# Crossbar transposes, v scaled on GpSimd, and a list-scheduled order, in a fused linear attention and squared-ReLU FFN

## The chip, the cores and the metric

One core of a Trainium2 chip. The metric is the device time of one execution in microseconds. A run is called slow when it lies over 1.5% above the fastest run of the same kernel; only fast runs are compared here unless it is said otherwise. Engines: PE is TensorE, ACT is ScalarE, DVE is VectorE, POOL is GpSimd, SP is the sync engine, which here only issues DMAs.

## The reference

The attention is linear, with a feature map of two exponentials. Its output is the FFN's input.

```python
# q, k, v: (8, 8, 576, 64); w_phi: (64, 128); w_in: (512, 2048); w_out: (2048, 512)
def phi(x):
    proj = np.einsum('bhsd,df->bhsf', x, w_phi)
    proj = proj - np.max(np.abs(proj), axis=-1, keepdims=True)
    return np.concatenate([np.exp(proj), np.exp(-proj)], axis=-1)
q_p, k_p = phi(q), phi(k)
kv = np.einsum('bhsf,bhsd->bhfd', k_p, v);  z = np.sum(k_p, axis=2)
num = np.einsum('bhsf,bhfd->bhsd', q_p, kv)
den = np.einsum('bhsf,bhf->bhs', q_p, z)[..., None] + 1e-06
x = (num / den).transpose(0, 2, 1, 3).reshape(4608, 512)
h = np.maximum(x @ w_in, 0.0);  return (h * h) @ w_out
```

## The kernel before

Attention runs batch by batch (8 batches of 576 tokens), the FFN chunk by chunk (9 chunks of 512 tokens). The FFN of chunk c is merged, in program order, with the attention of batch c + 1. Per batch, attention does this: load k, q and v with a cast to bf16 (POOL); transpose k and q on PE through one PSUM buffer; project; take the absolute maximum (DVE) and the exponentials of k (ACT); scale v by exp of the maximum (DVE); accumulate kv; build the features of q with the maximum subtracted by a small matmul; divide; transpose x on PE; copy x^T out of PSUM (ACT).

```python
for tg in tgroups:                                    # k and q: PE transpose, DVE copy
    for x, xt, tag in ((xk, kT, "kT"), (xq, qT, "qT")):
        tp = ps.tile([P, 2, 512], BF16, tag="tp", bufs=1, name="tp")
        ...
                nc.tensor.transpose(out=dst, in_=src, identity=ident)
        nc.vector.tensor_copy(out=t[:, : len(tg), :w], in_=tp[:, : len(tg), :w])
...
nc.vector.tensor_copy(out=mp[:, :, 0:NI], in_=mq)     # the split of the maximum of q
nc.vector.tensor_tensor(
    out=mp[:, :, NI : 2 * NI], in0=mq, in1=mp[:, :, 0:NI], op=ALU.subtract)
...
    nc.vector.tensor_tensor(                          # v scaled
        out=o[:, :, :, :D], in0=v0,
        in1=o[:, :, :, D].to_broadcast([P, 4, 4, D]), op=ALU.mult)
...
    nc.tensor.transpose(                              # x
        out=xtp[:, c, :m], in_=xo[:m, c * P : (c + 1) * P], identity=ident[:m, :m])
nc.scalar.activation(out=xT[ch][:, :, col : col + m], in_=xtp[:, :, :m], func=ACT.Copy)
...
def ffn_in(c, mc):                                    # 16 per chunk
    ... 4 matmuls of 128x512 ...
    nc.scalar.activation(out=hr, in_=hp, func=ACT.Relu)
    nc.vector.tensor_tensor(out=t, in0=hr, in1=hr, op=ALU.mult)
...
for c in range(NCH + 1):
    ...
    merge(a, 44, steps(ffn_units(c)), 16 if c in (0, NCH) else 32)
```

## Time and profile before

| | before |
|---|---|
| median of 4 runs | 458.7 us (458.1 to 459.3) |
| PE / DVE / ACT / POOL busy | 394.7 / 267.1 / 252.0 / 34.0 us of 457.1 |
| first FFN matmul | 54.9 us |
| PE busy from 120 to 320 us | 182.8 of 200 us |

The first fence has lines of the profile's page of the kernel before: busy time of each engine with its share of the span and its instructions; then the span in 40 slices of 11.4 us, where a digit is the busy share in tenths (PEclk is the granted PE clock in tenths of full speed); then the chain of work that ended last, by engine.

```profile
PE 394.7 (86%) x4320; PEld 211.2 (46%) x4376; DVE 267.1 (58%) x465; ACT 252.0 (55%) x377; POOL 34.0 (7%) x58
...
PE   0646799799888998899899989998999899999975
...
PEclk9996599999999999999999999999999999999999
DMA  8999514410641154116412540110111112021122
...
PE 49%; DVE 29%; ACT 14%; issue 4%; DMA 2%; POOL 1%; ACTq 0%; another core or an unknown queue 0%; DVEq 0%; POOLq 0%
```

The second is the busy time by windows. After the window come its length and the busy time of PE, PE weight loads, DVE, ACT and POOL, each with its number of instructions, then the granted clock, the DMA share and GB/s.

```profile
core 0: us, PE busy (x) PEld busy (x) DVE busy (x) ACT busy (x) POOL busy (x), PEclk, DMA share, GB/s
0.00:50.00 50.00, 23.74 (x358) 17.01 (x358) 24.13 (x36) 19.79 (x25) 15.60 (x28) 0.89 1.10 189
50.00:100.00 50.00, 44.38 (x528) 24.13 (x535) 31.36 (x55) 31.12 (x49) 3.66 (x6) 0.91 0.30 51
120.00:320.00 200.00, 182.83 (x2293) 99.03 (x2321) 137.29 (x237) 128.55 (x193) 12.31 (x20) 1.00 0.28 52
```

PE is what the kernel is bound by, once it has started: from 120 to 320 us it is busy for 182.8 of 200 us. (Of 4376 matmuls, as the weight loads count them, 4320 are recorded, so busy times of PE may be a few us low; FFN matmuls without gaps come every 0.22 us, so 28 missing in these 200 us are up to 6.) In the first 50 us it works less than half of the time, because batch 0's attention has nothing to be merged with.

The third is DVE's timeline where batch 0 splits the maximum of q: two instructions of 0.2 us.

```profile
27.74 0.18 DVE L175 CAST mpack_95<-mq 128x36 bf16<-128x36 f32 x1
27.96 0.20 DVE L176 TENSOR_TENSOR mpack_95<-mq,mpack_95 128x36 bf16<-128x36 f32 x1
```

### The profile page before, as it was taken

To read this page: it belongs to the slowest core of one execution; us is meant where nothing else is said; L and a number is where in the kernel's file an instruction comes from. 1 tells how busy PE (TensorE), PEld (TensorE's weight loads), DVE (VectorE), ACT (ScalarE), POOL (GpSimd) and SP (SyncE) were. 2 spreads that over 40 slices of the span, in tenths; PEclk is the share of its full clock that TensorE was granted. 3 is DMA by queue.
4 is the path that set the end of the run, shared out by engine and by line. 5 is a ranking of instruction groups with operands and counts; after the bars stand their busy time and mean duration, and the time that the engine had idled before them with its cause. 6 is when DMAs were issued, how large, how long until landed. Compare 5 with 4: busy or idle time off the path is not lost.

```text
span 457.1 us, 9984 instructions
## 1 busy us (share of the span) xinstructions
PE 394.7 (86%) x4320; PEld 211.2 (46%) x4376; DVE 267.1 (58%) x465; ACT 252.0 (55%) x377; POOL 34.0 (7%) x58
## 2 busy tenths in 40 slices
PE   0646799799888998899899989998999899999975
PEld 0434454555455545454555455545554554444432
DVE  2881279628953895389547963796469643333221
ACT  1445458466856574747674757485738474333300
POOL 8220020102010201020102010000000000000000
PEclk9996599999999999999999999999999999999999
DMA  8999514410641154116412540110111112021122
GB/s 121 215 204 207 91 25 81 77 24 10 113 81 24 22 107 77 24 30 123 76 24 40 112 65 13 33 39 1 24 24 24 26 24 47 23 48 25 45 46 68
DMA packets 21612, 28.47 MB, mean 62 GB/s; under 512 B 2112, under 2 KB 16448, under 8 KB 21568
## 3 DMA queue, kind: packets, MB, share of 16 engines
q0 software_dynamic: 15808, 18.39, 24.9%
q1 hardware_dynamic: 5760, 9.44, 8.5%
q8 instruction: 34, 0.56, 0.5%
q14 instruction: 10, 0.08, 0.1%
HBM read 36.77 MB, written 9.44 MB: 101 GB/s over the span
## 4 chain that ended last, share of the span: by engine, by line
PE 49%; DVE 29%; ACT 14%; issue 4%; DMA 2%; POOL 1%; ACTq 0%; another core or an unknown queue 0%; DVEq 0%; POOLq 0%
PE op L331 18%; PE hp L312 16%; DVE mk L153 5%; PE wide L280 4%; DVE mq L153 4%; DVE vp L202 4%; DVE vn L202 4%; ACT hr L317 3%; DVE xo L289 3%; ACT qp L242 3%; PE tp L129 3%; ACT qn L242 3%; PE xtp L297 2%; PE wide L144 2%; PE wide L258 2%
## 5 line engine op out<-in xcount | busy, mean ns | idle before, releaser
L312 PE MATMUL hp<-xT,win 128*128 128x512 bf16 x546 | 150.0, 383 | 2.8 <-issue 1.6
L317 ACT ACTIVATE hr<-hp 128x512 bf16<-128x512 f32 x144 | 86.0, 607 | 83.3 <-PE hp L312 72.4
L312 PEld LDWEIGHTS <-win 128*128 128x128 bf16 x576 | 52.0, 98 | 55.6 <-issue 2.1
L165 ACT ACTIVATE kp<-wide 128x1024 bf16<-128x1024 f32 (+1 forms) x40 | 37.5, 939 | 36.3 <-DVE mk L153 36.1
L242 ACT ACTIVATE qp<-wide 128x1024 bf16<-128x1024 f32 (+1 forms) x40 | 37.5, 937 | 34.2 <-PE wide L228 34.2
L153 DVE TENSOR_REDUCE mk<-wide 128x8 f32<-128x1024 f32 (+1 forms) x40 | 44.5, 1113 | 4.6 <-PE wide L144 4.6
L153 DVE TENSOR_REDUCE mq<-wide 128x8 f32<-128x1024 f32 (+1 forms) x40 | 44.4, 1110 | 0.5 <-PE wide L144 0.4
L337 DVE COPY ot<-op 128x512 f32<-128x512 f32 x36 | 24.8, 688 | 29.7 <-PE op L331 28.3
L242 ACT ACTIVATE qn<-wide 128x1024 bf16<-128x1024 f32 (+1 forms) x40 | 37.6, 941 | 0.0
L166 ACT ACTIVATE kn<-wide 128x1024 bf16<-128x1024 f32 (+1 forms) x40 | 37.5, 938 | 0.0
L280 PE MATMUL wide<-kv_sb,qp 128*128 128x65 bf16 (+1 forms) x320 | 31.8, 200 | 2.9 <-ACT qp L242 2.9
L287 DVE RECIPROCAL rden<-wide 128x8 f32<-128x8 f32 (+1 forms) x40 | 8.1, 204 | 42.7 <-PE wide L280 42.4
L280 PE MATMUL wide<-kv_sb,qn 128*128 128x65 bf16 (+1 forms) x320 | 26.8, 200 | 4.4 <-ACT qn L242 4.2
L280 PEld LDWEIGHTS <-qp 128*128 128x128 bf16 (+1 forms) x320 | 23.9, 103 | 12.7 <-ACT qp L242 8.4
L280 PEld LDWEIGHTS <-qn 128*128 128x128 bf16 (+1 forms) x320 | 23.2, 104 | 14.2 <-ACT qn L242 13.2
L289 DVE TENSOR_TENSOR xo<-wide,rden 128x512 bf16<-128x512 f32 (+1 forms) x40 | 27.5, 689 | 1.2
L303 ACT ACTIVATE xT<-xtp 128x512 bf16<-128x512 bf16 (+1 forms) x40 | 22.1, 552 | 4.7 <-PE xtp L297 4.3
L266 ACT ACTIVATE kv_sb<-wide 128x520 bf16<-128x520 f32 x16 | 9.4, 604 | 23.4 <-PE wide L258 23.4
L297 PE MATMUL xtp<-ident,xo 128*128 128x128 bf16 (+1 forms) x160 | 15.9, 225 | 7.0 <-DVE xo L289 6.1
L144 PE MATMUL wide<-wphi_70,kT 64*128 64x128 bf16 x288 | 16.6, 229 | 4.9 <-DVE mq L153 4.4
L67 POOL DMA_DIRECT2D xk<-in_k_dram x16 | 10.1, 637 | 144.2 <-PE tp L129 80.4
L129 PE MATMUL tp<-ident,xk 128*128 128x128 bf16 (+1 forms) x160 | 13.1, 231 | 8.7 <-POOL ident masks.py:199 8.1
(481 smaller groups left out, 612.6 us busy)
## 6 DMA issues: line engine op xcount, KB each, us to landing
out_dram<-ot SPq DMA_DIRECT2D x72, 128.0 KB, 2.4
xk<-in_k_dram POOLq DMA_DIRECT2D x16, 288.0 KB, 4.9
xq<-in_q_dram POOLq DMA_DIRECT2D x16, 288.0 KB, 6.6
xv<-in_v_dram POOLq DMA_DIRECT2D x16, 288.0 KB, 5.5
win<-in_moe_w_in_dram POOLq DMA_DIRECT2D x1, 2048.0 KB, 18.1
wout<-in_moe_w_out_dram POOLq DMA_DIRECT2D x1, 2048.0 KB, 28.7
wphi_70<-in_w_phi_dram POOLq DMA_DIRECT2D x2, 16.0 KB, 1.9
```

The lines of the kernel that those rows point to most:

```text
L129: nc.tensor.transpose(out=dst, in_=src, identity=ident)
L144: nc.tensor.matmul(out=pj[:, e, i * Fd : (i + 1) * Fd], lhsT=xt[r, i * P : (i + 1) * P], rhs=wphi2[r, :], start=True, stop=True,)
L153: nc.vector.tensor_reduce(out=m[:, :, at : at + w], in_=pj[:, :, : w * Fd].rearrange("x e (i f) -> x e i f", f=Fd), axis=AX.X, op=ALU.max, ...
L165: nc.scalar.activation(out=kp[:, :, :w], in_=pj[:, :, :w], func=ACT.Exp, scale=1.0)
L166: nc.scalar.activation(out=kn[:, :, :w], in_=pj[:, :, :w], func=ACT.Exp, scale=-1.0)
L202: nc.vector.tensor_tensor(out=o[:, :, :, :D], in0=v0, in1=o[:, :, :, D].to_broadcast([P, 4, 4, D]), op=ALU.mult,)
L242: nc.scalar.activation(out=o, in_=i_, func=ACT.Exp, scale=sg)
L280: nc.tensor.matmul(out=ndv[:m, h, : D + 1], lhsT=qph[s][:, h, :m], rhs=kv_sb[:, s, h % 2, h // 2, :], start=(s == 0), stop=(s == 1),)
L289: nc.vector.tensor_tensor(out=xo[:m].rearrange("t (h d) -> t h d", h=8), in0=ndv[:m, :, :D], in1=rden[:m].to_broadcast([m, 8, D]), op=ALU. ...
L312: nc.tensor.matmul(out=hp, lhsT=win[:, kc, mc * P : (mc + 1) * P], rhs=xT[c][:, kc, :], start=(kc == 0), stop=(kc == KC1 - 1),)
L317: nc.scalar.activation(out=hr, in_=hp, func=ACT.Relu)
L331: nc.tensor.matmul(out=op, lhsT=h2[c, mc][:, tt * P : (tt + 1) * P], rhs=wout[:, mc, :], start=(mc == 0), stop=(mc == KC2 - 1),)
```

## The change

The intent: take all transposes but a tiny one off PE, with their PSUM buffer and their copies (DVE for q and k, ACT for x); take v's scaling off DVE; and let a list scheduler in the kernel, with a cost for each operation, fix the order on every engine, so that the attention of two batches overlaps the FFN. A token order (pr, j) makes the transposes plain, and all buffers are static.

```diff
-                        nc.tensor.transpose(out=dst, in_=src, identity=ident)
-                nc.vector.tensor_copy(out=t[:, : len(tg), :w], in_=tp[:, : len(tg), :w])
+                    nc.sync.dma_start_transpose(
+                        out=xt.t[:, u0 // 2 : (u0 + n) // 2, :],
+                        in_=xb.t[:, u0 : u0 + n, :].rearrange("x u d -> x (u d)"),
+                    )
 ...
-                nc.vector.tensor_tensor(out=o[:, :, :, :D], in0=v0, ...)
+                    nc.gpsimd.tensor_tensor(
+                        out=t.t[:, us, :D], in0=xv.t[:, us, :],
+                        in1=t.t[:, us, D].to_broadcast([P, M, D]), op=ALU.mult)
 ...
-                nc.tensor.transpose(out=xtp[:, c, :m], ...)
-            nc.scalar.activation(out=xT[ch][:, :, col : col + m], in_=xtp[:, :, :m], func=ACT.Copy)
+                    nc.sync.dma_start_transpose(out=xT.t[:, tt], in_=xo.t)
 ...
+    r_xk = ring("xk", 1, [P, U, D], BF16)         # was two buffers
+    r_xq = ring("xq", 1, [P, U, D], BF16)         # was two buffers
+    r_wide = ring("wide", 2, [P, 2, 512], F32, ps)
 ...
+    def load(key, kb, fn, deps=(), bufs=()):
+        i = pl.op("pool", 650, key, fn, deps, bufs, lat=0)
+        return pl.op("dma", kb * 2.5, key, None, [i], bufs, lat=2200)
+    def xbar(key, kb, fn, deps=(), bufs=()):      # the list's costs in ns: 100 to issue, 4 per KB, 2300 to land
+        i = pl.op("sp", 100, key, fn, deps, bufs, lat=0)
+        return pl.op("xb", kb * 4, key, None, [i], bufs, lat=2300)
 ...
+    def place(b):                                 # a batch's attention over 64 FFN slots of the list;
+        if b == 0:                                # an FFN chunk is 32 slots
+            return lambda i: -200 + i
+        return lambda i: 32 * b - 24 - 64 * (1 - i / 100)
 ...
+        for o in pl.order():
+            if o.fn is not None:
+                o.fn()
```

## The prediction

> **What bounds the kernel now.** TensorE. The engine table gives PE busy 394.7 of 457.1 us, DVE 267.1, ACT 252.0, GpSimd 34.0; the chain of waits is 49% PE, 29% DVE, 14% ACT. Three stretches (busy time by windows, timeline of PE):
> - 0 to 55 us: batch 0's attention alone, a DVE/ACT latency chain, under loads that keep the DMA engines full (207 to 215 GB/s) to about 50 us. First FFN matmul at 54.9 us.
> - 55 to about 390 us: attention and FFN merged, PE 92% busy (147.3 of 160 us from 160 to 320), a batch about 45 us. The granted clock is 0.5 from 40 to 60 us, then 1.0.
> - the rest: FFN alone, 0.216 us per matmul.
>
> **What changes.**
> - Off PE: 480 transposes (xk, xq, xo). Eight take about 0.65 us warm (13.1 us busy for 160): some 30 us, and their waits (6.1 us on xo).
> - Off ACT: xT copies, 22 us. Off DVE: kT/qT copies 26.6 us, v scaling 45 us.
> - Added: 80 crossbar transposes of q and k, 36 of x, on the sync queue, 14 MB. [...] They fit the idle DMA time after 50 us; before it they share with the loads.
> - Added on GpSimd: 32 products of 128x1152. [...]
> - Moved: attention of two batches overlaps the FFN, without round trips through the single transpose PSUM buffer, and ends earlier; the FFN-only tail is about 75 us. FFN, projections, features, kv and num/den matmuls are unchanged.
>
> **Prologue.** PE's fixed order puts batch 1's first k projection before batch 0's numerators, and that load now comes after w_out. At 210 GB/s it lands at about 38 to 41 us[...]. The first FFN matmul stays at 50 to 57 us; I expect almost nothing here.
>
> **Sum.** FFN 1152 x 0.216 = 249 us; attention PE work of batches 1 to 7 about 7 x 10.3 = 72; start 54; end 3: 378 us with no stall. Before, the same sum with transposes was 406 and the run 457: 51 us lost to waits and clock. I expect 32 lost[...]. **Predicted 410 us, 8 in 10 between 388 and 438.** Faster by over 2%: 0.88; within: 0.08; slower: 0.04.
>
> **What would show it.** PE busy falls to 355 to 370 us, over 88% busy from 60 to 330 us; first FFN matmul between 50 and 57 us; DVE near 195 us[...]; PE's waits on transposes below 10 us in all.
>
> **What would make it wrong.** Transposes that land in 5 us or more would hold every projection and every chunk's first FFN matmul, in an order that cannot adapt. The fixed GpSimd order (loads behind products, products behind loads) could starve a batch. [...]

The sum in it is made of times from the profile before: 249 + 72 + 54 + 3 = 378 us with no stall. With 32 us for waits, the estimate from the 51 us lost before, it came to 410. Terms are cut from the text where a cut is marked, because no trace before the change showed them: the time of a crossbar transpose (which also stood in the estimate for the prologue), the length of a GpSimd product, and the squarings held by GpSimd, for which the author charged PE 10 to 20 of the 32 us, with the two totals that hung on them. "Warm" in it: eight transposes take 1.01 us at the start of the trace before (8.08 us) and 0.61 later (152.74).

## The result, and the profile after

The changed kernel takes 522.4 us (517.8 to 524.6, 4 runs, all fast), 1.138 times the time before (95% interval 1.129 to 1.146). Ratios are the mean time of one kernel's fast runs over that of the other's of the same rounds, so they are not quite the ratio of the medians.

| | before | after |
|---|---|---|
| median | 458.7 us | 522.4 us |
| PE / DVE / ACT / POOL busy | 394.7 / 267.1 / 252.0 / 34.0 us | 374.7 / 235.1 / 230.0 / 102.2 us |
| first FFN matmul | 54.9 us | 89.7 us |
| PE busy from 120 to 320 us | 182.8 us, clock 1.00 | 144.1 us, clock 0.85 |

The first FFN matmul: all w_in matmuls before (shortest, median and longest in ns, then the first and the last start: 54.9 and 433.6 us), and the first of them after (start, duration, engine, line, operation; in brackets what it waited for, in us):

```profile
L312 PE MATMUL hp<-xT,win x546: 376/379/634, 54.9 to 433.6; 128*128 128x512 bf16 x182
89.70 1.87 PE L484 MATMUL hp_146<-xT_106,win 128*128 128x512 bf16 x4 [5.86 <-DMA xT_106<-xo_103]
```

The same lines of the page of the kernel after (a slice is 13.0 us here):

```profile
PE 374.7 (72%) x3850; PEld 195.0 (37%) x3896; DVE 235.1 (45%) x368; ACT 230.0 (44%) x337; POOL 102.2 (20%) x90
...
PE   0002553779733866699647976899799899999996
...
PEclk9999999989955998789968997999899999999998
DMA  8999795532497216901684056903431031311123
...
PE 46%; ACT 14%; DMA 12%; DVE 12%; issue 8%; SPq 6%; POOL 1%; DVEq 0%; ACTq 0%; POOLq 0%
```

And the same windows:

```profile
0.00:50.00 50.00, 3.78 (x56) 2.56 (x57) 8.74 (x10) 7.21 (x7) 10.79 (x21) 1.00 1.07 168
50.00:100.00 50.00, 26.16 (x381) 17.68 (x377) 18.76 (x29) 22.64 (x30) 14.48 (x14) 1.00 0.73 116
120.00:320.00 200.00, 144.09 (x1623) 76.07 (x1637) 101.83 (x143) 97.27 (x143) 45.34 (x36) 0.85 0.48 79
```

Work did leave PE, DVE and ACT, but PE idles more than it saved: 3.8 us of work in the first 50, and 144 us from 120 to 320. The granted clock is 0.85 in that stretch; its lowest two slices (5 tenths) are those in which PE is busy for 3 tenths only. DMA and the sync queue are new in the chain of work that ended last (12% and 6%). From 400 us on, when loads and most of attention are over, PE is busy without gaps; so the loss lies before that.

Three places show what the new waits look like. The first is the sync queue at the start (start, duration, queue, line, operation; x5 is five transposes of batch 0, merged):

```profile
7.92 18.30 SPq L267 DMA_TRANSPOSE kT_71<-xk_67  x5
26.34 16.54 SPq L267 DMA_TRANSPOSE qT_72<-xq_68  x5
```

Ten transposes take 35 us, and this is the critical chain (start, duration, what) in that stretch:

```profile
9.33 1.49 SPq L267
...
10.86 7.30 SPq L267
...
18.20 6.71 SPq L267
...
30.47 14.70 DMA qT_72<-xq_68
```

The queue holds one transpose for 1.49 us (9.33; 1.2 to 1.5 in the second place below), the one after it for 7.30, the next for 6.71, and one of q lands 14.7 us after its issue (30.47). The five of k land 12.4 to 21.2 us after theirs. In these 50 us the DMA engines are full with the loads of the weights (the DMA line above: 8 and 9 tenths).

The second is batch 2, from 144 us, again the critical chain:

```profile
144.80 1.24 SPq L267
...
146.09 1.54 SPq L267
...
147.68 1.35 SPq L267
...
149.08 1.35 SPq L267
...
150.53 1.19 SPq L267
...
151.82 2.63 DMA xT_107<-xo_104
...
155.74 9.44 DMA xT_107<-xo_104
...
165.31 1.86 PE hp_146 L484 x4
```

Five transposes of k stand in the queue before the x transposes, for 6.9 us, then an x transpose lands after 9.44 us, and the FFN chunk (165.31) can only start behind it. POOL had issued the loads of the next batch at 154.7 us. Over all x transposes the landing goes from 2.4 to 10.3 us.

The third is DVE in batch 4, at the same two small instructions as before, and POOL beside them:

```profile
255.43 0.25 DVE L343 CAST mpack_98<-m_94 128x36 bf16<-128x36 f32 x1
255.71 9.12 DVE L344 TENSOR_TENSOR mpack_98<-m_94,mpack_98 128x36 bf16<-128x36 f32 x1
```

```profile
256.30 4.27 POOL L331 TENSOR_TENSOR va_86<-xv_69,va_86 128x1152 bf16<-128x1152 bf16 x2
260.51 4.26 POOL L331 TENSOR_TENSOR va_87<-xv_69,va_87 128x1152 bf16<-128x1152 bf16 x2
```

The subtraction, 0.2 us before, lasts 9.12 us: as long as all four products of POOL, which run from 256.3 to 264.8 (times on POOL are rough). This is the worst of eight: five of the others last 2.06 to 2.12 us, the length of one product, and two stay at 0.20. DVE does nothing else meanwhile, and the q features of that batch and the division of another wait.

So there are three candidates: the crossbar (beside loads, and in the queue), the products on GpSimd, and the order itself.

### The profile page after: what moved, and what is told of

It is laid out like the page before. It is cut to its first block, busy times and chain, and to the rows that moved or that the text cites. A ratio compares the mean times of both kernels' runs of the same rounds, so it can differ in the third digit from the quotient of the medians.

```text
span 521.8 us, 9278 instructions
## 1 busy us (share of the span) xinstructions
PE 374.7 (72%) x3850; PEld 195.0 (37%) x3896; DVE 235.1 (45%) x368; ACT 230.0 (44%) x337; POOL 102.2 (20%) x90
## 3 DMA queue, kind: packets, MB, share of 16 engines
HBM read 36.77 MB, written 9.44 MB: 89 GB/s over the span
## 4 chain that ended last, share of the span: by engine, by line
PE 46%; ACT 14%; DMA 12%; DVE 12%; issue 8%; SPq 6%; POOL 1%; DVEq 0%; ACTq 0%; POOLq 0%
PE hp_146 L484 10%; PE hp_147 L484 9%; PE op_148 L506 8%; PE op_149 L506 7%; SPq L267 6%; DVE m_96 L289 3%; DMA qT_72<-xq_68 3%; DMA xT_106<-xo_104 3%; ACT qph_92 L416 3%; DMA xT_108<-xo_105 2%; DMA xT_107<-xo_104 2%; DVE m_95 L289 2%; ACT qph_93 L416 2%; PE wide_145 L445 2%; PE wide_145 L372 2%
## 5 line engine op out<-in xcount | busy, mean ns | idle before, releaser
L219 POOL DMA_DIRECT2D xq_68<-in_q_dram x16 | 9.9, 628 | 186.2 <-DMA qT_72<-xq_68 109.9
L484 PE MATMUL hp_146<-xT_107,win 128*128 128x512 bf16 x96 | 26.2, 398 | 9.7 <-DMA xT_107<-xo_104 8.0
L445 PEld LDWEIGHTS <-qph_92 128*128 128x128 bf16 (+1 forms) x320 | 28.0, 116 | 13.3 <-issue 10.9
L445 PEld LDWEIGHTS <-qph_93 128*128 128x128 bf16 (+1 forms) x320 | 27.4, 114 | 13.2 <-issue 12.2
L484 PE MATMUL hp_146<-xT_106,win 128*128 128x512 bf16 x96 | 26.9, 406 | 6.3 <-DMA xT_106<-xo_103 5.9
L283 PEld LDWEIGHTS <-kT_71 64*128 64x128 bf16 x288 | 10.2, 101 | 55.7 <-DMA kT_71<-xk_67 28.3
L488 ACT ACTIVATE hr_110<-hp_146 128x512 bf16<-128x512 f32 x24 | 14.8, 616 | 34.1 <-PE hp_146 L484 34.1
L484 PE MATMUL hp_146<-xT_108,win 128*128 128x512 bf16 x96 | 26.3, 399 | 4.6 <-DMA xT_108<-xo_105 4.6
L283 PE MATMUL wide_144<-wphi_61,kT_71 64*128 64x128 bf16 x144 | 8.5, 239 | 29.1 <-DMA kT_71<-xk_67 21.9
L331 POOL TENSOR_TENSOR va_86<-xv_70,va_86 128x1152 bf16<-128x1152 bf16 x8 | 17.0, 2148 | 57.6 <-ACT va_86 L326 57.6
L484 PE MATMUL hp_147<-xT_106,win 128*128 128x512 bf16 x96 | 26.4, 400 | 0.2 <-ACT hr_111 L488 0.2
L331 POOL TENSOR_TENSOR va_86<-xv_69,va_86 128x1152 bf16<-128x1152 bf16 x8 | 17.1, 2161 | 47.1 <-ACT va_86 L326 47.1
L488 ACT ACTIVATE hr_111<-hp_146 128x512 bf16<-128x512 f32 x24 | 14.7, 614 | 26.1 <-PE hp_146 L484 26.1
L484 PE MATMUL hp_147<-xT_107,win 128*128 128x512 bf16 x96 | 25.6, 390 | 0.3 <-ACT hr_109 L488 0.2
L484 PE MATMUL hp_147<-xT_108,win 128*128 128x512 bf16 x96 | 25.5, 390 | 0.0
L488 ACT ACTIVATE hr_109<-hp_146 128x512 bf16<-128x512 f32 x24 | 14.8, 616 | 23.6 <-PE hp_146 L484 22.3
L289 DVE TENSOR_REDUCE m_94<-wide_144 128x8 f32<-128x1024 f32 (+1 forms) x14 | 15.0, 1070 | 20.8 <-PE wide_144 L283 19.6
L416 ACT ACTIVATE qph_92<-wide_144 128x1024 bf16<-128x1024 f32 (+1 forms) x22 | 20.9, 952 | 2.7 <-PE wide_144 L409 2.7
L513 DVE COPY ot_142<-op_148 128x512 f32<-128x512 f32 x18 | 12.4, 689 | 21.4 <-PE op_148 L506 21.4
L513 DVE COPY ot_143<-op_149 128x512 f32<-128x512 f32 x18 | 12.4, 688 | 20.7 <-PE op_149 L506 20.7
L416 ACT ACTIVATE qph_93<-wide_144 128x1024 bf16<-128x1024 f32 (+1 forms) x22 | 21.1, 961 | 0.0
```

What stands on the lines that cost most here:

```text
L219: nc.gpsimd.dma_start(out=buf.t[hi * 64 : hi * 64 + 64].rearrange("p (pr j) d -> p pr (j d)", j=NJ), in_=rows[hi],)
L283: nc.tensor.matmul(out=w.t[:, e, i * Fd : (i + 1) * Fd], lhsT=xt.t[r, u0 // 2 + i, :], rhs=wphi2[r, :], start=True, stop=True,)
L289: nc.vector.tensor_reduce(out=mb.t[:, :, u0 // 2 : (u0 + n) // 2], in_=w.t[:, :, : n * 64].rearrange("x e (i f) -> x e i f", f=Fd), axis=A ...
L331: nc.gpsimd.tensor_tensor(out=t.t[:, us, :D], in0=xv.t[:, us, :], in1=t.t[:, us, D].to_broadcast([P, M, D]), op=ALU.mult)
L416: nc.scalar.activation(out=qph[s].t[:, :, :, u0 * 32 : (u0 + n) * 32].rearrange("f hi e c -> f e hi c"), in_=w.t[:, :, : n * 64].rearrange ...
L445: nc.tensor.matmul(out=nd[lo:hi_, h, : D + 1], lhsT=qph[s].t[:, h % 2, u % 2, c0 : c0 + hi_ - lo], rhs=kv[h // 4][0].t[:, h % 2, h // 2 % ...
```

## The experiments

Every kernel here gave a correct result, unless it is said that it is wrong. Where transposes are "on TensorE" in the list order, they go through one PSUM buffer with a DVE copy for q and k and an ACT copy for x, as before; the second PSUM buffer of the FFN's output is given up for it. All these runs, and the crossbar run of experiment 6 on the 438 us kernel, also claim both feature buffers of k before a projection, which the change does not (`two = [Buf(r_kph), Buf(r_kph)]`); no run separates that.

### 1. The parts apart, in the order of the change

TensorE transposes in the list order, v on GpSimd:

```diff
+    r_op = ring("op", 1, ...);  r_tp = ring("tp", 1, [P, 8, P], BF16, ps)
-                    nc.sync.dma_start_transpose(out=xt.t[...], in_=xb.t[...])
+                        nc.tensor.transpose(out=w.t[:, i, :], in_=xb.t[...], identity=ident)
+                d_ = dve(..., nc.vector.tensor_copy(out=xt.t[...], in_=w.t[...]))
-                    nc.sync.dma_start_transpose(out=xT.t[:, tt], in_=xo.t)
+                        nc.tensor.transpose(out=w.t[:, c_, :], in_=xo.t[...], identity=ident)
+                act(..., nc.scalar.activation(out=xT.t[:, tt], in_=w.t[...], func=ACT.Copy))
```

> The list order with all transposes (q, k, x) back on TensorE through one PSUM bank, v still scaled on GpSimd. Theory A (the crossbar is the cost: slow landings beside loads, and 1.2 us of sync queue per transpose in an order that planned 0.1): 425 to 450 us, first FFN matmul near 55 us. Theory B (GpSimd products that hold up VectorE are the cost): still 490 us or more. Theory C (the fixed order itself is the cost, whatever runs in it): still 490 or more.

The same, and v on VectorE, so that of the change the order, the token layout and the static buffers are left:

```diff
-                    nc.gpsimd.tensor_tensor(
+                    nc.vector.tensor_tensor(
```

> The list order alone: transposes on TensorE and v scaled on VectorE, as before, with the flat token order and static buffers kept. A: 420 to 445 us. B: about 440 to 460. C: 480 or more, that is, slower than before although all operations are those of before.

The change with only v put back on VectorE (the same one-line edit, crossbar kept):

> The changed kernel with v scaled on VectorE, crossbar kept. A: 490 to 515 us, the first FFN matmul still at about 85 to 90 us, and the x transposes that run beside loads still land in 9 to 10 us. B: 450 to 470 us. C: about 520. In all, the longest split subtraction on VectorE should drop from 9.1 us to about 0.2.

Measured in the same rounds (before: 458.3 us), medians of four fast runs:

| list order, 64 slots | v on VectorE | v on GpSimd |
|---|---|---|
| transposes on TensorE | 480.9 (1.051) | 496.6 (1.085) |
| transposes on the crossbar | 491.6 (1.072) | 522.4 (1.138, the change; its own rounds) |

None of the three theories stands alone. The order by itself, with every operation on its old engine, costs 22.6 us (480.9 less 458.3). GpSimd adds 15.7 to that, the crossbar 10.8, and both together 41.5, which is 15.0 more than the two alone.

Where the time goes shows when each profiled run is split at its first FFN matmul:

| us to the first FFN matmul, and from there to the end | v on VectorE | v on GpSimd |
|---|---|---|
| transposes on TensorE | 63.9 and 415.0 | 68.2 and 426.8 |
| transposes on the crossbar | 85.5 and 405.4 | 89.7 and 432.1 |

The crossbar costs 21.5 us before the FFN starts in both columns. After that it gains 10 us with v on VectorE, and costs 5 with v on GpSimd: the 15.0 of "both together" lie after the first FFN matmul.

Theory A (the crossbar is the cost) had expected 420 to 445 for the order alone, so it fell; so did B and C as the only cause. In the run with v on VectorE the subtraction is back at 0.196 us (mean of 8), and the x transposes still take up to 9.7 us to land.

### 2. The crossbar without load traffic

The change, in the same order on PE, ACT and SP, with nearly no loads (the two memsets are added work on VectorE); the result is wrong:

```diff
-nc.gpsimd.dma_start(out=win, in_=win_v)
-nc.gpsimd.dma_start(out=wout, in_=wout_v)
+nc.gpsimd.dma_start(out=win[:, :, :128], in_=win_v[:, :, :128])
+nc.gpsimd.dma_start(out=wout[:, :1, :], in_=wout_v[:, :1, :])
+        nc.vector.memset(win[:, :, 128:], 0.02);  nc.vector.memset(wout[:, 1:, :], 0.02)
 ...
+                nd = NJ * D if b < 2 else D          # k, q, v of batches 2 to 7: a ninth
```

> The changed kernel in the same order on TensorE, ScalarE and the sync queue, but with nearly no load traffic: w_in and w_out loads cut to a sixteenth (the rest set to a constant), the loads of batches 2 to 7 cut to a ninth. Wrong result on purpose. A: crossbar landings fall to 2.4 us everywhere, first FFN matmul before 60 us, total 445 to 470 us. B and C: little changes after the prologue; total above 490.

It takes 476.3 us (1.040; 2 runs, wrong result), 46 us less than the change. The sync queue in the window shown above:

```profile
8.45 7.87 SPq L268 DMA_TRANSPOSE kT<-xk  x5
16.44 8.77 SPq L268 DMA_TRANSPOSE qT<-xq  x5
29.80 6.67 SPq L268 DMA_TRANSPOSE kT<-xk  x5
37.47 7.03 SPq L268 DMA_TRANSPOSE qT<-xq  x5
```

Ten transposes now take 16.6 us instead of 35, still beside batch 0's and 1's own loads, and the first FFN matmul is at 69.7 us instead of 89.7. No x transpose takes over 4.2 us to land (10.3 before). Without the loads, 46 of the change's 64 us are gone: 20 us of it before the first FFN matmul, the rest later. This is not all the crossbar's: putting the transposes back on TensorE takes away 25.8 us (522.4 less 496.6). The run also removes every wait for the loads themselves, and no run without loads was made with transposes on TensorE, so the split of the 46 stays open. The expectation of a first FFN matmul before 60 us was missed: even alone, five transposes in a row hold the queue for about 7 us, and the order adds its part. The rate at which the queue issues q and k undisturbed can be worked out from 6.67 us for the 590 KB of one tensor: 88 GB/s.

### 3. Fewer, larger transposes

```diff
-            for g, (u0, n) in enumerate(GRP):                # 4, 4, 4, 4 and 2 blocks
+            for u0, n in ((0, U),):                          # 18 blocks at once
```

> The changed kernel with one crossbar transpose per tensor (18 blocks) in place of five (4, 4, 4, 4, 2), so 16 instead of 80 of them for q and k. If the sync queue's 1.2 us is a cost per instruction, the queue gives 16 x 1.2 instead of 80 x 1.2 us to them, x transposes no longer stand 13 us behind them, and the total falls to 500 to 512 us. If it is a cost per block, one instruction takes 5 us or more and the total stays at 515 to 530. Either way the prologue stays near 90 us, since what holds it is the load traffic.

It takes 525.2 us (1.143): no gain. The queue is held by six of the eight merged transposes of k for 2.3 to 3.6 us each, against 6.7 for five; the line gives the shortest, the median and the longest in ns:

```profile
L267 SPq DMA_TRANSPOSE kT<-xk x8: 2316/3070/9588, 8.0 to 364.8; - x8
```

So most of the queue's 1.2 us is a cost per instruction (in the kernel after, the queue takes 1.20 us for four blocks at 246.11 us, and 1.20 for two at 251.33), and the list's 0.1 us for it was wrong. But the total did not fall. Two things speak against a gain: with loads in the way the longest transpose of k still held the queue for 9.6 us and one of q for 25.3, and each tensor lands as a whole, 4.5 us after its issue at the earliest against 2.3. That these ate what the shorter queue gave is argued and not shown.

### 4. Single parts in the order of before

GpSimd alone (both product instructions of v; one is shown):

```diff
-                nc.vector.tensor_tensor(out=o[:, :, :, :D], in0=v0, ...)
+                nc.gpsimd.tensor_tensor(out=o[:, :, :, :D], in0=v0, ...)
```

> The kernel before with v scaled on GpSimd, nothing else changed. If a GpSimd product holds VectorE's two-input instructions (split subtraction of 0.2 us and squarings of 0.43 us) until a run of them ends, some of those last 2 to 9 us here as well, and the total is 470 to 485 us, since the products (2.1 us per 128x1152) also stand in the chain between the absmax and the kv matmuls, at twice VectorE's time. If the lock only bites in the list order, 455 to 465.

It takes 504.5 us (1.101), 46 us more than before, and more than the 470 to 485 expected. PE waits 39.8 us for the scaled v (12.8, 9.6, 9.6 and 7.8 in the table of waits), and the mean squaring on VectorE goes from 0.43 to 0.54 us.

The crossbar for x alone:

```diff
-            nc.scalar.activation(out=xT[ch][:, :, col : col + m], in_=xtp[:, :, :m], func=ACT.Copy)
+            nc.sync.dma_start_transpose(out=xT[ch][:, :, col : col + m], in_=xo[:m, :])
```

> The kernel before with only the x transposes on the crossbar. It takes 160 matmuls off TensorE (about 10 us) and 22 us off ScalarE. If landings of 2.4 us alone and 9 to 10 us beside loads hold here too, and every chunk's first FFN matmul waits for the last of them: 462 to 480 us. If the old order hides them: 445 to 455.

It takes 455.3 us (0.994, 95% interval 0.991 to 0.996), at the upper end of "the old order hides them": 3 us gained, although 160 matmuls left PE. PE waits 12.3 us for x transposes in all, and the first FFN matmul comes at 62.3 us instead of 54.9: here too the crossbar loses before the FFN and gains after it.

### 5. What is wrong with the order

In the list order with all operations on their old engines, ACT does this at 190 us, when a batch's q features meet the next batch's projections:

```profile
190.59 1.02 ACT L319 ACTIVATE kph<-wide 128x1024 bf16<-128x1024 f32 x1 [1.29 <-DVE m L298]
191.51 1.93 ACT L426 ACTIVATE qph<-wide 128x1024 bf16<-128x1024 f32 x2
193.32 1.11 ACT L504 ACTIVATE hr<-hp 128x512 bf16<-128x512 f32 x2
194.28 1.07 ACT L319 ACTIVATE kph<-wide 128x1024 bf16<-128x1024 f32 x1
```

Each k exponential (kph) waits behind two q exponentials (qph) and two ReLUs (hr), and each holds one of the two wide PSUM buffers that the next projection needs; from 196.6 us the same sequence comes again. A batch's attention is spread over 64 slots of the list and the next one starts 32 slots later, so its second half, with the q exponentials, lies on the next one's first half, with the k exponentials. The test changes two constants: the spread, and the number of buffers for loaded k and q (before had two; the list had one, so batch 1's loads waited for batch 0's transposes behind the weight loads, 27.2 us in the chain of that run).

```diff
-        return lambda i: 32 * b - 24 - 64 * (1 - i / 100)
+        return lambda i: 32 * b - 24 - 44 * (1 - i / 100)
-    r_xk = ring("xk", 1, ...);  r_xq = ring("xq", 1, ...)
+    r_xk = ring("xk", 2, ...);  r_xq = ring("xq", 2, ...)
```

> The list order with all operations on their engines of before (481 us), with two constants changed: one batch's attention spread over 44 FFN slots in place of 64, so that the q exponentials of one batch no longer lie on the k projections of the next, and a second buffer for xk and xq, so that batch 1's loads need not wait for batch 0's transposes. If the overlap of the two exp-heavy phases and the late load are what makes the list order slower than before: 435 to 455 us, first FFN matmul at 55 to 58 us instead of 64. If the list order is slow for another reason (its fixed order itself): 475 to 485.

It takes 437.9 us (0.956, 95% interval 0.954 to 0.958). It beats both kernels, with the operations of before on their engines of before. PE from 120 to 320 us:

```profile
120.00:320.00 200.00, 195.88 (x2363) 105.96 (x2357) 141.34 (x237) 136.84 (x204) 9.85 (x16) 1.00 0.29 53
```

That is 195.9 of 200 us, against 182.8 before, of which up to 6 may be missing records. ACT around 195 us has k exponentials, x copies and ReLUs, and the q exponentials only start at 201:

```profile
192.31 1.02 ACT L319 ACTIVATE kph<-wide 128x1024 bf16<-128x1024 f32 x1 [0.60 <-PE wide L292]
193.23 0.59 ACT L483 ACTIVATE xT<-tp 128x512 bf16<-128x512 bf16 x1
...
196.90 1.08 ACT L319 ACTIVATE kph<-wide 128x512 bf16<-128x512 f32 x2 [0.28 <-DVE m L298]
...
201.06 1.94 ACT L426 ACTIVATE qph<-wide 128x1024 bf16<-128x1024 f32 x2
```

To split the two constants, the spread alone:

> The list order with all operations on their engines of before and attention spread over 44 slots in place of 64, but single xk and xq buffers as in the change. It splits the gain of the 438 us kernel from the 481 us one. If the spread (which phases of two batches lie on each other) gives most of it: 440 to 450 us, first FFN matmul still at 62 to 65. If the second buffers give most: 465 to 475.

It takes 451.8 us (0.986), 29 less than with 64 slots; its first FFN matmul stays at 64.1 us. The second buffers bring that to 51.9 us and give the other 14. The spread was slightly above its 440 to 450; both constants matter.

That the spread is worth 29 us is shown; that it is so because k exponentials stand behind q exponentials is shown for a small part only. From 120 to 320 us, PE waits 3.2 us for k exponentials with 64 slots and 0.6 with 44. Its largest wait with 64 slots is another, 5.7 us for kv matmuls behind the division of x on VectorE. PE is idle for 17.2 us there with 64 slots, at a granted clock of 0.95, and for 3.7 with 44, at 1.00. Which of the overlaps that the spread makes costs what stays open.

### 6. The parts again, in the good order

The change itself with these two constants:

> The changed kernel as it is (crossbar, v on GpSimd), with the two constants of the 438 us kernel: 44 slots and second xk and xq buffers. If the spread alone were what was wrong: 440 to 455 us. If crossbar beside loads and GpSimd products cost as much in a good order as in the bad one (41 us there): 475 to 495 us. The first FFN matmul should stay at 75 to 95 us, since batch 0's transposes still stand beside the weight loads.

Its four runs took 493.1, 501.4, 502.1 and 502.7 us, so by the rule only the run of 493.1 us is fast, and there is no interval. With 493 to 503 us against 437.9 the crossbar and GpSimd together cost at least 55 us here. Its first FFN matmul came at 100 us, in the profile of a slow run (502.1 us).

The 438 us kernel with all transposes on the crossbar:

> The 438 us kernel with all transposes on the crossbar (v stays on VectorE). If only load contention of the crossbar costs: first FFN matmul at 75 to 90 us instead of 52, little lost after it or even some gained (28 us less TensorE work): 445 to 465 us. If it costs in the merged stretch too: 465 to 480 us.

It takes 465.1 us (1.016), 27.2 more. The first FFN matmul comes at 85.5 us instead of 51.9, 33.6 later:

```profile
85.51 1.89 PE L485 MATMUL hp<-xT,win 128*128 128x512 bf16 x4
```

From there to the last w_in matmul it takes 357.7 us, against 360.6 in the 438 us kernel. In this order the crossbar costs its time before the FFN starts, and gains 3 us after that.

The 438 us kernel with v on GpSimd:

> The 438 us kernel with v scaled on GpSimd (transposes stay on TensorE). In the order of before this cost 46 us, in the list order with 64 slots 16 us. If GpSimd's products cost by holding VectorE's split subtraction and squarings, which no order avoids while the split follows the same projections as the products: 448 to 462 us. If a good order hides them: 435 to 444.

It takes 454.4 us (0.991), 16.5 more: as in the poor order.

### 7. Crossbar only away from the weight loads

Transposes on TensorE for batches 0 and 1, on the crossbar for 2 to 7 (both forms as above, chosen by `if b >= 2` for q and k, `if b < 2` for x):

> The 438 us kernel with batches 0 and 1 on TensorE transposes and the crossbar for q, k and x of batches 2 to 7. The crossbar in all batches cost 27 us in this order, with the first FFN matmul at 85.5 us instead of 51.9. If only the prologue beside the weight loads costs: first FFN matmul at 50 to 54 us, total 428 to 438 us. If the crossbar also costs in the merged stretch: 442 to 460.

It takes 438.0 us (0.955), the same as without any crossbar. The cost is gone with the prologue's transposes, and the gain is nothing, although transposes left PE: the whole kernel has some 320 fewer matmuls there. From 120 to 320 us PE is busy for 178.8 us instead of 195.9 (26 matmuls are missing from this record, which is up to 6 us), so it idles more: its two largest waits in the whole run, both for ACT's exponentials, are 21.2 us together and 13.2 in the 438 us kernel. What PE was given it does not use.

Only x on the crossbar, in all batches:

> The 438 us kernel with only the x transposes on the crossbar, in all batches. In the kernel before this alone gave 3 us. If x transposes meet loads only now and then: 432 to 440 us, first FFN matmul at 52 to 58. If their slow landings beside loads hold the chunks: 445 to 460.

It takes 455.2 us (0.993), 17 more than with none: 9 of them before the first FFN matmul (60.8 us). This was above the range for "only now and then", and why x alone costs more here than q, k and x do in batches 2 to 7 above is not settled: the list made a different order for each, and no run separates that.

### 8. Is it GpSimd's hold on VectorE, or only a slower engine?

The 438 us kernel with the 32 products on GpSimd once more, into a scratch tile that nobody reads. Orders on all engines but POOL are the same:

```diff
+                    nc.gpsimd.tensor_tensor(
+                        out=dum[:, us, :], in0=xv.t[:, us, :],
+                        in1=t.t[:, us, D].to_broadcast([P, M, D]), op=ALU.mult)
```

> The 438 us kernel with v scaled on VectorE as there, plus the same 32 products on GpSimd once more, into a scratch tile that nobody reads. Orders on TensorE, VectorE, ScalarE and the sync queue are identical to that kernel's. If what costs is that a GpSimd product holds VectorE's two-input instructions: mean squaring 0.55 to 0.65 us, v products on VectorE stretched too, total 450 to 465 us. If what costs is only that GpSimd takes 2.1 us where VectorE takes 1.36, in the chain: 436 to 442 us.

And the same with GpSimd writing only, 32 memsets of 2.0 us:

```diff
-                    nc.gpsimd.tensor_tensor(out=dum[:, us, :], ...)
+                    nc.gpsimd.memset(dum, 0.0)
```

> As the run with dummy products, but GpSimd only writes (32 memsets of 128x2304 into the scratch tile) and reads nothing. If it is reading the SBUF that holds VectorE: squarings stay at 0.42 us and the total at 436 to 440. If any GpSimd work holds VectorE: longer squarings, 445 or more.

The products that nobody waits for (in the trace only POOL itself waits for them) bring it to 491.1 us (1.071), 53 more, above both expectations; the memsets leave it at 437.2 us (0.954). The groups of VectorE (line, engine, operation, names, shapes, count, busy us, mean ns), first with the extra products, then with the memsets:

```profile
L342 DVE TENSOR_TENSOR va<-xv,va 128x1152 bf16<-128x1152 bf16 x32 | 96.7, 3066 | 0.5 <-ACT va L337 0.4
...
L514 DVE TENSOR_TENSOR h<-hr 128x512 bf16<-128x512 bf16 x144 | 64.7, 458 | 57.5 <-ACT hr L511 56.7
```

```profile
L512 DVE TENSOR_TENSOR h<-hr 128x512 bf16<-128x512 bf16 x144 | 59.2, 419 | 58.1 <-ACT hr L509 57.2
L342 DVE TENSOR_TENSOR va<-xv,va 128x1152 bf16<-128x1152 bf16 x32 | 41.8, 1354 | 0.5 <-ACT va L337 0.4
```

VectorE's own v products, which run at the same time, go from 1.35 to 3.07 us on average; with the memsets nothing moves. The memsets are not quite the same test: they wait for nothing, so most run earlier than VectorE's v products (the last starts at 266.5 us, the last extra product at 393.1). But 19 squarings and three v products did run beside a memset, and no squaring in that run took over 0.43 us and no v product over 1.37. (The profile of the first run fell in a slow execution, 497.6 us; its fast ones took 490.0 to 491.1.) So in these runs GpSimd's products, which read, hold VectorE (v products 3.07 us against 1.35), and its memsets, which only write, do not (1.35); and this costs time, 53 us, even where nobody waits for its results. The cast before the split, with one input, is held too when it meets products: 1.29 us on average in the first run of experiment 1, against 0.16 in the second. The size, 53 us, is that of a worst case, since these products meet VectorE's on purpose; v scaled on GpSimd itself cost 16 us in this order, and there the mean squaring went from 0.419 to 0.635 us.

## Why the prediction was wrong

- **The bound, right.** PE is the main engine of the chain in both kernels (49% and 46%), and its busy time fell by the transposes, though to 374.7 us, above the expected 355 to 370.
- **The prologue, wrong: the step that failed first.** The prediction counted a short landing for each transpose, noted that before 50 us they share with the loads, and still left the first FFN matmul at 50 to 57 us: "I expect almost nothing here". It came at 89.7. Alone, transposes land in 2.4 us; beside the weight loads those of k took up to 21.2 us, the chain shows 14.7 us for one of q, and 7 us to issue one. Of the 35 us, 21.5 come with the crossbar, about 9 with the order and the single buffers (63.9 us with no crossbar), and 4 with GpSimd (experiment 1). The prediction had named landings of 5 us or more among what would make it wrong, and did not count them.
- **The order, wrong in sign.** The prediction took 51 us of waits and clock before and expected the list to leave 32. The list with all old operations costs 22.6 us instead. Spreading attention over 64 slots laid the second half of one batch on the first half of the next; 44 slots and second buffers give 437.9 us. That a list order can cut the waits was right, but not this list.
- **GpSimd, mechanism right, size too small in the change.** The prediction charged PE 10 to 20 us for squarings held by GpSimd's products; this was the author's estimate, and no trace before the change showed such a hold. Without the crossbar, the parts show 15.7 and 16.5 us in the two list orders (4 to 5 of it before the first FFN matmul, where there are no squarings to hold); in the change, beside the crossbar, it is 30.8 (522.4 less 491.6), and 46 in the order of before. That two of these fall within 10 to 20 is partly luck. The hold itself experiment 8 shows: beside the extra products VectorE's v products took 3.07 us against 1.35 and the mean squaring 0.458 against 0.419, both with inputs in SBUF, while the reductions out of PSUM stayed at 1.11 us; beside memsets nothing changed. What was missed is that the split of q's maximum follows the same projections as the products, so in the 64-slot order it is hit by schedule and not by chance: six of the eight subtractions in the change. (With 44 slots and no crossbar only one was, and the squarings were hit instead.) A product on GpSimd took 2.15 us.
- **Crossbar in the merged stretch, wrong together with GpSimd.** "They fit the idle DMA time after 50 us" is true of the bytes, and not of the moments: the loads of a batch are issued right behind its products, which is when the x transposes of another batch are due (9.44 us). After the first FFN matmul the crossbar costs 5 us in the change, where it should have gained; with v on VectorE it does gain 10 there (experiment 1). In the 44-slot order it costs nothing after batch 1, but it gains nothing either (experiment 7).
- **The sum.** 378 us with no stall plus 32 was 410; the run was 522. In the list's order of 64 slots the 64 us over before are 22.6 (order) + 15.7 (GpSimd) + 10.8 (crossbar) + 15.0 (both together). The last term was not in the prediction at all, and all of it lies after the first FFN matmul; a possible cause is that GpSimd's products and the loads behind them shift the moments at which transposes and loads meet, which is argued and not shown.

## What to carry to other kernels

Count a transfer's cost at the moment it runs, not on average: a crossbar transpose that takes 2.4 us alone took up to 21.2 us beside bulk loads, and in this kernel those loads are densest exactly where nothing else hides it. Before moving elementwise work to GpSimd, look at the VectorE instructions that fall at the same time, above all small ones in a critical chain: here a subtraction of 0.20 us was held for up to 9.12 us, and the mean squaring went from 0.419 to 0.635 us, while reductions out of PSUM stayed at 1.11. And when a list fixes an order, try how far apart it puts the phases of two batches before moving any work: here two constants were worth 43 us, and moving transposes or products off their engines never gained more than the 3 us of experiment 4.
